# Rotated mixed-chunk keys, 64-column last AV products, spread weight units and later 1/sum transposes in a fused attention and MoE kernel

## Chip, cores and metric

The kernel runs on one core of one Trainium2 chip. The metric is device time in microseconds (us), the median of the runs shown. Times inside a run come from one profiled execution, whose own total is given beside its span.

## What is computed

An attention layer with a learned position bias, followed by two mixture layers. Cut to what matters:

```python
# q, k, v: (4, 8, 576, 64) = batch B, heads H, sequence S, head size D, float32
scores = q @ k.T / 8 + bias                    # bias: a small network of |i-j| and i, one map for each head
attn = exp(scores - max) ; attn /= sum(attn) + 1e-9
x = attn @ v                                   # reshaped to 2304 tokens of 512
h = x @ w_in;  x = (h * relu6(h + 3) / 6) @ w_out             # 512 -> 2048 -> 512
out = (sigmoid(x @ w_gate) * (x @ w_val)) @ w_out2            # 512 -> 1536 -> 512
```

## The kernel before

**Stages.** First the bias maps are built and put in DRAM (lines 540 to 590). Then comes the attention loop (lines 625 to 638), then the two feed-forward layers (from line 650). One unit `n` of attention is a pair of heads of one batch element, so there are 16 units (`NU`).

**Steps and slots.** A unit has nine steps `s` (`NSTEP`). The 576 queries of a head are cut into four chunks of 128 and a rest of 64. Steps 0 to 7 do one chunk `c = s // 2` of one head `h = s % 2`; step 8 does the rests of both heads together, 64 rows each, and is called the mixed chunk here. `slot_of_two(i)` (L463) writes down the work of two steps at a time, and of earlier slots: the scores of slot i, AV products that are due, the exponentials of slot i, `invert` of slot i-1, `turn_inv` of slot i-2, the transposes of slot i-1, and the preparation of the next unit's queries and keys (`prep`, mostly on POOL). The builder then orders each engine's queue itself by readiness and this order, with `tc.issue_after` as an added edge on one engine, so in the trace neighbouring slots interleave.

**One step.** `scores` (L333) makes two halves of 288 keys in one PSUM tile: each half is the sum of two products with a 128x128 query tile as weights, one for the high part of the keys and one for the low part (`r`), and in step 8 of four, as both heads add into one tile (L342). DVE adds the bias and takes the row minimum in one instruction (L346). ACT takes the exponential and the row sum (L362) into `pts`, or for step 8 into `Pm`.

**Transposes.** `trans` (L394) turns the probabilities key-major, four 128x128 blocks into one PSUM tile `tr` (L400; a ring of three), and ACT or DVE evicts them to `ptm`. Head 0 takes keys 0 to 511 this way, head 1 keys 64 to 575. For the mixed chunk the two heads lie in different row halves and start at different columns, so it takes four 64x64 blocks for each head in a `tr` tile of its own, and two evictions (L404 to L410). The 64 keys that are left of each head go through `trans_rem` (L412) into `ptr`: one 128x128 block for each chunk (L415), and two more for the mixed chunk (L418, L419). `Pm` has 64 columns of zeros ahead for this.

**AV.** `av(n, a, g)` (L424) makes the output for 288 queries (`a`). For `g` 0 to 3 there is a product of 64 weight columns for each head, into partitions 0 to 63 and 64 to 127 of one PSUM tile (L432). For `g` 4 one product of 128 weight columns does both heads (L435): the first 64 columns of `v` hold zeros in the rows of the other head, and so on. Each of these plain float32 products shows as two MATMULs in the trace; the scores are float32r and show as one. `av_out` (L437) multiplies by `inv`, with the one PSUM buffer `av`.

**1/sum.** `invert` (L365) adds 1e-9 to the row sums (L368), takes the reciprocal (L369) and spreads it (ACT, L373), after steps 5 and 8. `turn_inv` (L375) transposes that into a `tr` tile (L379) and evicts it to `inv`.

**Weights.** The first ten weight tiles of the next layer are made ready during attention. `load.whole` (L229), in slots 12, 18, ..., 66 (L633), writes down for one tile the DMA of its raw 64-bit words (L159), the absolute value on ACT (L175), four operations on DVE (L176, L184, L186, L188), a copy on ACT (L192) and a subtraction on POOL (L193).

## Time and profile before

| | us |
|---|---|
| median of 3 runs | 1158.08 |
| lowest and highest run | 1157.95, 1161.23 |
| profiled execution, its own time | 1160.52 |
| its span, first to last instruction | 1158.7 |

The mean granted TensorE clock is 0.998 of full speed. Over the span PE is busy for 1135.9 us (98%), weight loads 1012.2 (87%), DVE 772.8 (67%), ACT 588.4 (51%) and POOL 422.6 (36%). The attention loop lies at about 56 to 340 us. PE and PEld are the matmuls and the weight loads of TensorE. A view by line gives the number of instructions, their summed busy time and the mean length of one; as matmuls overlap in the array, the mean is longer than the step from one to the next. The chain of waits gives each piece only the time that it added, and so is read for steps.

### The profile page before, as it was taken

Reading aid. Unit: us, or ns where it says so; the run is one execution under the profiler, and the core shown is the slowest. Engines: PE = TensorE matmul, PEld = TensorE weight load, DVE = VectorE, ACT = ScalarE, POOL = GpSimd, SP = SyncE. Lnnn points to the kernel's source line nnn. Section 1 sums busy time; section 2 is a strip of 40 time slices with the busy share of each in tenths; the row PEclk is TensorE's granted clock in tenths of the full one; section 3 lists DMA queues with packets and bytes.
Section 4 is the critical chain, followed back from the end, with each engine's and each line's share of the span. In section 5 each row is a group of like instructions: output and inputs, shape, how many; then the busy total and the mean of one; then the engine's idle time right before and its main releaser. Section 6 shows DMA issues by size and latency. Waiting matters only on the chain.

```text
span 1158.7 us, 19146 instructions
## 1 busy us (share of the span) xinstructions
PE 1135.9 (98%) x6862; PEld 1012.2 (87%) x6862; DVE 772.8 (67%) x1495; ACT 588.4 (51%) x1296; POOL 422.6 (36%) x342
## 2 busy tenths in 40 slices
PE   8799999999999999999999999999999999999998
PEld 3277777777779999999999999999899898998997
DVE  8977878788868887355386775585367655644443
ACT  7988887877855545454455454342333222221221
POOL 0154544544316433232347445261333223311211
PEclk9999999999999999999999999999999999999999
DMA  6854436353213665249467759976878848757532
GB/s 203 298 162 110 158 95 183 112 165 103 78 55 110 209 218 200 101 174 340 167 228 255 253 189 357 395 261 251 308 254 309 311 165 299 285 181 258 191 109 73
DMA packets 83183, 236.82 MB, mean 204 GB/s; under 512 B 9616, under 2 KB 12304, under 8 KB 83088
## 3 DMA queue, kind: packets, MB, share of 16 engines
q1 hardware_dynamic: 83088, 235.60, 58.6%
q8 instruction: 54, 0.88, 0.3%
q14 instruction: 41, 0.34, 0.1%
HBM read 154.15 MB, written 81.41 MB: 203 GB/s over the span
## 4 chain that ended last, share of the span: by engine, by line
PE 84%; DVE 6%; ACT 2%; DMA 2%; issue 1%; POOL 1%; SPq 0%; POOLq 0%; DVEq 0%; ACTq 0%
PE o L673 17%; PE h L807 10%; PE o L807 10%; PE s L342 6%; PE o L862 6%; PE h L862 5%; PE h L611 5%; PE h L610 5%; PE h L612 5%; PE av L432 5%; PE tr L400 4%; PE av L435 1%; DVE z L186 1%; DVE u L346 1%; PE tr L379 1%
## 5 line engine op out<-in xcount | busy, mean ns | idle before, releaser
L673 PE MATMUL o<-gh,slot 128*128 128x384 f32 x768 | 196.0, 336 | 1.8 <-DVE take L392 1.8
L673 PEld LDWEIGHTS o<-gh,slot 128*128 128x128 f32 x768 | 139.2, 188 | 2.3 <-DVE take L392 2.1
L673 PE MATMUL o<-gl,slot 128*128 128x384 f32 x384 | 129.1, 336 | 0.7 <-DVE gl L659 0.7
L362 ACT ACTIVATE p<-u,stat 128x576 f32<-128x576 f32 x128 | 98.7, 773 | 29.2 <-DVE stat L346 28.4
L342 PE MATMUL s<-k,q 128*128 128x288 f32 x640 | 111.0, 309 | 0.7 <-ACT ptm L557 0.4
L346 DVE CUSTOM_DVE_ANT_0 u<-s,bias 128x576 f32<-128x576 f32 x128 | 93.6, 753 | 24.4 <-PE s L342 23.2
L843 POOL TENSOR_TENSOR gp<-s,gp 128x384 fp32r<-128x384 f32 x36 | 39.4, 1107 | 177.0 <-ACT gp L842 92.6
L617 DVE SCALAR_TENSOR_TENSOR g<-g,h 128x384 f32<-128x384 f32 x94 | 51.6, 549 | 70.2 <-ACT g L616 70.1
L659 DVE TENSOR_TENSOR gl<-g,gh 128x384 fp32r<-128x384 f32 x94 | 63.1, 671 | 48.3 <-ACT gh L658 45.8
L658 ACT CAST gh<-g 128x384 fp32r<-128x384 f32 x94 | 48.3, 513 | 91.6 <-DVE g L617 91.3
L193 POOL TENSOR_TENSOR hl<-corners,hl 128x512 fp32r<-128x512 f32 x42 | 57.2, 1366 | 94.3 <-ACT hl L192 79.3
L342 PEld LDWEIGHTS s<-k,q 128*128 128x128 f32 x640 | 88.8, 189 | 2.3 <-ACT ptm L557 0.6
L616 ACT ACTIVATE g<-h,half 128x384 f32<-128x384 f32 x94 | 54.3, 578 | 58.4 <-PE h L612 57.9
L807 PE MATMUL o<-x,slot 128*128 128x384 f32 x432 | 78.4, 336 | 1.4 <-DVE sum L787 1.4
L432 PE MATMUL av<-ptm,vn 128*64 128x288 f32 x512 | 77.8, 419 | 0.7 <-DVE x L444 0.7
L807 PE MATMUL h<-x,slot 128*128 128x384 f32 x432 | 77.8, 335 | 0.0
L807 PEld LDWEIGHTS o<-x,slot 128*128 128x128 f32 x432 | 75.1, 188 | 2.0 <-DVE sum L787 1.7
L807 PEld LDWEIGHTS h<-x,slot 128*128 128x128 f32 x432 | 75.2, 188 | 0.7
L400 PE MATMUL tr<-ident,p 128*128 128x128 f32 x512 | 72.2, 275 | 2.2 <-ACT inv L390 1.5
L673 PEld LDWEIGHTS o<-gl,slot 128*128 128x128 f32 x384 | 72.5, 189 | 1.3 <-DVE gl L659 1.3
L314 POOL TENSOR_TENSOR k<-early,one 128x576 fp32r<-128x576 f32 x30 | 34.4, 1167 | 106.3 <-DVE x L572 53.1
L843 POOL TENSOR_TENSOR x<-s,x 128x384 fp32r<-128x384 f32 x36 | 40.3, 1129 | 84.2 <-ACT x L842 50.5
(157 smaller groups left out, 2725.2 us busy)
## 6 DMA issues: line engine op xcount, KB each, us to landing
w<-hl SPq DMA_DIRECT2D x67, 512.0 KB, 3.3
slot<-w SPq DMA_DIRECT2D x67, 512.0 KB, 5.8
raw<-in_part_dram SPq DMA_DIRECT2D x50, 512.0 KB, 4.1
x<-xc SPq DMA_DIRECT2D x56, 384.0 KB, 6.0
sum<-sum SPq DMA_DIRECT2D x72, 256.0 KB, 3.5
early<-xc SPq DMA_DIRECT2D x28, 384.0 KB, 6.4
nbias<-ptm SPq DMA_DIRECT2D x36, 295.5 KB, 3.1
early<-in_part_dram SPq DMA_DIRECT2D x32, 288.0 KB, 4.3
```

Of the source, the lines that this page charges most:

```text
L342: last_s[0] = nc.tensor.matmul(ps[:, a, 0:HS], Q[:, q0 : q0 + P], K[:, r, h, HS * a : HS * a + HS], start=(i == 0), stop=(i == len(mm) - 1))
L346: last_u[0] = nc.vector.tensor_tensor_reduce(out=halves(u), in0=ps[:, :, 0:HS], in1=halves(bt), op0=ALU.add, op1=ALU.min, scale=-0.125, sc ...
L362: nc.scalar.activation(probs(t), us.pop(t), AF.Exp, bias=low[n % 2][:, s : s + 1], scale=-1.0, accum_out=sums[n % 3][:, s : s + 1])
L400: nc.tensor.transpose(ps[:, kc], pts[n, c][:, h, 64 * h + P * kc : 64 * h + P * kc + P], ident)
L432: nc.tensor.matmul(ps[64 * h : 64 * h + 64, 0:HS], vt[:, 4 * h + g], ptm[:, h, g, cols], start=(g == 0), stop=False)
L610: nc.tensor.matmul(ps[:, 0:TW], wh, XH[:, c], start=(c == 0), stop=False)
L611: nc.tensor.matmul(ps[:, 0:TW], wl, XH[:, c], start=False, stop=False)
L659: last_g[0] = nc.vector.tensor_tensor(out=gl, in0=g, in1=gh.bitcast(F32), op=ALU.subtract)
L673: nc.tensor.matmul(os[c][:, 0:TW], sl[:, r, P * c : P * c + P], x, start=(first and r == 0 and x is gh), stop=(last and x is gl))
L807: nc.tensor.matmul(ps[b], sl[:, r, o : o + P], x[:, c, s], start=(k < 4 and i == 0), stop=(i == len(mm) - 1), skip_group_check=True)
L843: nc.gpsimd.tensor_tensor(out=G[:, i, 1], in0=s, in1=G[:, i, 0].bitcast(F32), op=ALU.subtract)
L862: nc.tensor.matmul(os[i], x[:, P * i : P * i + P], slots[(base + 14 + e) % NALL][:, r], start=first, stop=last)
```

## The change

There are five edits. The loop has 76 slots (`NSLOT`), the last four only to finish.

1. The bias rows of the mixed chunk's second head are loaded with keys 64 to 575 first and keys 0 to 63 last, and `scores` writes its products in this order (`keys`). In half `a` = 1 a product of 288 keys of head 1 becomes one of 224 and one of 64.
2. With both heads' keys in the same columns, `trans` takes four 128x128 blocks for the mixed chunk, one `tr` tile and one eviction, on DVE and ACT in turn by unit; `trans_rem` takes one block more in place of two, and `Pm` loses its zero columns and their memsets.
3. `av` with `g` = 4 does a product of 64 weight columns for each head.
4. A weight tile's work is spread over six slots from slot 9(m+1)//2 on (`one_step`): DMA; absolute value and maximum; shift; one merge; the other merge; copy and subtraction. The ten tiles start in slots 4, 9, 13, ..., 45.
5. `turn_inv` comes one slot later and first in its slot, and 1e-9 is added as a two-input operation with a tile `tiny`.

```diff
 NPRE = 10
-EVERY = 6
 PRIME = (NU * NSTEP // 2 - 2, NU * NSTEP // 2 + 1)
...
     one = keep.tile([P, 1], F32, name="one")
+    tiny = keep.tile([P, 1], F32, name="tiny")
     slots = [keep.tile([P, 2, 512], F32R, name=f"slot{i}") for i in range(NPRE)]
...
 
+        def shift(self, i):
+            z = self.z[i][0].bitcast(I32)
+            nc.vector.tensor_scalar(out=z, in0=z, scalar1=3, scalar2=0x3FFFFFF8, op0=ALU.logical_shift_left,
+                                    op1=ALU.bitwise_and)
+
+        def merge(self, i, w):
+            z, raw = self.z[i]
+            z = z.bitcast(I32)
+            scalar, op = ((29, ALU.logical_shift_right), (-0x40000000, ALU.bitwise_and))[w]
+            nc.vector.scalar_tensor_tensor(out=z, in0=raw[..., w], scalar=scalar, in1=z, op0=op, op1=ALU.bitwise_or)
+
         def assemble(self, i):
...
             self.raw.pop(i)
-            z, raw = self.z[i]
-            zi = z.bitcast(I32)
-            nc.vector.tensor_scalar(out=zi, in0=zi, scalar1=3, scalar2=0x3FFFFFF8, op0=ALU.logical_shift_left,
-                                    op1=ALU.bitwise_and)
-            nc.vector.scalar_tensor_tensor(out=zi, in0=raw[..., 1], scalar=-0x40000000, in1=zi,
-                                           op0=ALU.bitwise_and, op1=ALU.bitwise_or)
-            nc.vector.scalar_tensor_tensor(out=zi, in0=raw[..., 0], scalar=29, in1=zi,
-                                           op0=ALU.logical_shift_right, op1=ALU.bitwise_or)
+            self.shift(i)
+            self.merge(i, 1)
+            self.merge(i, 0)
 
...
 
-        def whole(self):
-            i = self.n
-            for stage in (self.dma, self.magnitude, self.assemble):
-                stage(i)
-            self.finish(i, nc.gpsimd)
-            self.n += 1
+        def one_step(self, i, k):
+            if k == 0:
+                self.dma(i)
+            elif k == 1:
+                self.magnitude(i)
+                self.raw.pop(i)
+            elif k == 2:
+                self.shift(i)
+            elif k < 5:
+                self.merge(i, 4 - k)
+            else:
+                self.finish(i, nc.gpsimd)
+                self.n = i + 1
 
...
     Ks = [apool.tile([P, 2, 2, S], F32R, name=f"k{i}") for i in range(2)]
-    Pm = [apool.tile([P, S + 64], F32, name=f"pm{i}") for i in range(2)]
+    Pm = [apool.tile([P, S], F32, name=f"pm{i}") for i in range(2)]
     ident = apool.tile([P, P], F32, name="ident")
...
             o = bias_t[c][:, h] if c < 4 else bias_m[64 * h : 64 * h + 64]
-            nc.sync.dma_start(o, rows_of[:, RK * (2 * p + h) : RK * (2 * p + h) + S])
+            i = rows_of[:, RK * (2 * p + h) : RK * (2 * p + h) + S]
+            if c == 4 and h == 1:
+                nc.sync.dma_start(o[:, 0:512], i[:, 64:S])
+                nc.sync.dma_start(o[:, 512:S], i[:, 0:64])
+            else:
+                nc.sync.dma_start(o, i)
 
...
 
+    def keys(s, h, a):
+
+        if s < 8 or h == 0:
+            return [(HS * a, 0, HS)]
+        return [(64, 0, HS)] if a == 0 else [(64 + HS, 0, HS - 64), (0, HS - 64, 64)]
+
     def scores(t):
...
         for a in range(2):
-            mm = [(h, c, r) for h, c in todo for r in range(2)]
-            for i, (h, c, r) in enumerate(mm):
+            mm = [(h, c, r, part) for h, c in todo for r in range(2) for part in keys(s, h, a)]
+            for i, (h, c, r, (k0, o, w)) in enumerate(mm):
                 q0 = (0, S + P)[h] + P * c if c < 4 else (512, S)[h]
-                last_s[0] = nc.tensor.matmul(ps[:, a, 0:HS], Q[:, q0 : q0 + P], K[:, r, h, HS * a : HS * a + HS],
-                                 start=(i == 0), stop=(i == len(mm) - 1))
+                last_s[0] = nc.tensor.matmul(ps[:, a, o : o + w], Q[:, q0 : q0 + P], K[:, r, h, k0 : k0 + w],
+                                             start=(i == 0), stop=(i == len(mm) - 1))
         u = a2.tile([P, S], F32, name="u", bufs=3)
...
             return pts[n, c][:, h]
-        return Pm[n % 2][:, 64:]
+        return Pm[n % 2]
 
...
         r = sums[n % 3][:, 2 * c0 : min(2 * c1, NSTEP)]
-        nc.vector.tensor_scalar(out=r, in0=r, scalar1=1e-9, scalar2=None, op0=ALU.add)
+        nc.vector.tensor_tensor(out=r, in0=r, in1=tiny.to_broadcast(r.shape), op=ALU.add)
         nc.vector.reciprocal(r, r)
...
         else:
-            pm = Pm[n % 2]
-            for h in range(2):
-                ps = pp.tile([P, 4, P], F32, name="tr", bufs=3)
-                r = slice(64 * h, 64 * h + 64)
-                for kc in range(4):
-                    nc.tensor.transpose(ps[:, kc, 0:64], pm[r, 64 + 64 * h + P * kc : 64 + 64 * h + P * kc + P],
-                                        ident[r, r])
-                evac("AV"[h], ptm[:, h, :, 512:S], ps[:, :, 0:64])
+            ps = pp.tile([P, 4, P], F32, name="tr", bufs=3)
+            for kc in range(4):
+                nc.tensor.transpose(ps[:, kc], Pm[n % 2][:, P * kc : P * kc + P], ident)
+            evac("VA"[n % 2], ptm[:, :, :, 512:S], ps.rearrange("p c (h q) -> p h c q", h=2))
 
...
         if c == 3:
-            pm = Pm[n % 2]
-            nc.tensor.transpose(ps[:, 1], pm[:, 0:P], ident)
-            nc.tensor.transpose(ps[0:64, 2], pm[:, S : S + 64], ident)
-            evac("A", ptr[0:64, 512:S], ps[0:64, 2, 0:64])
-            evac("V", ptr[64:P, 512:S], ps[64:P, 1, 64:P])
+            nc.tensor.transpose(ps[0:64, 1], Pm[n % 2][:, 512:S], ident)
+            for h in range(2):
+                evac("AV"[h], ptr[64 * h : 64 * h + 64, 512:S], ps[0:64, 1, 64 * h : 64 * h + 64])
         evac("A", ptr[:, P * c : P * c + P], ps[:, 0])
...
         else:
-            nc.tensor.matmul(ps[:, 0:HS], vt[:, 8:10].rearrange("p a d -> p (a d)"), ptr[:, cols], start=False, stop=True)
+            for h in range(2):
+                nc.tensor.matmul(ps[64 * h : 64 * h + 64, 0:HS], vt[:, 8 + h], ptr[:, cols], start=False, stop=True)
 
...
 
+        for t in steps(i - 3):
+            n, s = seq[t]
+            if s in (5, 8):
+                turn_inv(n, s // 6 * 3, s // 6 * 2 + 3)
         for t in steps(i):
...
                 invert(n, s // 6 * 3, s // 6 * 2 + 3)
-        for t in steps(i - 2):
-            n, s = seq[t]
-            if s in (5, 8):
-                turn_inv(n, s // 6 * 3, s // 6 * 2 + 3)
         for t in steps(i - 1):
...
         nc.vector.memset(one, 1.0)
+        nc.vector.memset(tiny, 1e-9)
         nc.scalar.activation(low[0][:, 0:1], one, AF.Relu)
...
         make_identity(nc, ident)
-        for i in range(2):
-            nc.gpsimd.memset(Pm[i][:, 0:64], 0.0)
 
...
                 begun[f] = hardswish(ring("z")[:, 0:TW], project(0, slots[2 * f], pp.tile([P, 2, 512], F32, name="s")[:, 0]))
-            if i % EVERY == 0 and i > 10 and load.n < NPRE:
-                with tc.issue_after(last_v[0].ins):
-                    load.whole()
+            for m in range(NPRE):
+                at = i - NSTEP * (m + 1) // 2
+                if 0 <= at <= 5:
+                    with tc.issue_after(last_v[0].ins):
+                        load.one_step(m, at)
             if i in PRIME:
...
 

```

## Rows read from the trace of the kernel before

**Rows 1.** Busy time by stretch: PE, PEld, DVE, ACT, POOL, clock, DMA share, GB/s
```profile
73.00:340.00 267.00, 264.19 (x1948) 201.52 (x1946) 209.37 (x540) 210.25 (x551) 121.88 (x92) 1.00 0.40 118
```
**Rows 2.** The page's chain that ended last, by engine
```profile
PE 84%; DVE 6%; ACT 2%; DMA 2%; issue 1%; POOL 1%; SPq 0%; POOLq 0%; DVEq 0%; ACTq 0%
```
**Rows 3.** Instructions by line and shape, PE, 56 to 346 us (busy us, mean ns | idle before)
```profile
L435 PE MATMUL av<-ptr,vn 128*128 128x288 f32 x64 | 24.1, 458 | 0.0
...
L408 PE MATMUL tr<-ident,pm 64*128 64x64 f32 x128 | 10.9, 235 | 0.0
```
**Rows 4.** Chain of waits, 200 to 230 us: AV and its neighbours (start us, us, what)
```profile
200.07 1.02 PE tr L400 x8
...
202.26 0.64 PE av L432 x4
202.90 0.68 PE av L435 x2
203.58 0.87 PE tr L400 x8
...
224.95 1.61 PE av L432 x12
```
**Rows 5.** Chain of waits, 69 to 76 us: mixed chunk transposed in one go
```profile
73.25 0.41 PE tr L408 x8
73.65 0.26 PE tr L415
73.91 0.11 PE tr L418
74.02 0.11 PE tr L419
```
**Rows 6.** Chain of waits, 200 to 230 us: eight whole score products, then a mixed chunk in two goes
```profile
223.90 1.06 PE s L342 x8
...
227.48 0.39 PE tr L408 x4
227.87 0.72 PE s L342 x4
228.59 0.39 PE tr L408 x4
228.98 0.33 PE s L342
229.31 0.11 PE tr L415
...
229.64 0.40 PE s L342 x3
```
**Rows 7.** Who PE waited for, 56 to 346 us (us in total, times, longest)
```profile
PE tr L400 <- ACT inv L390: 1.5, 3, 0.5
PE av L432 <- DVE x L444: 0.7, 3, 0.2
PE tr L400 <- DVE ptm L392: 0.6, 3, 0.2
```
**Rows 8.** Timeline, 122 to 131 us: a merge on DVE beside POOL
```profile
126.39 1.41 POOL L318 TENSOR_TENSOR q<-early,q 64x576 fp32r<-64x576 f32 x1 [2.22 <-ACT q L310]
...
126.44 1.92 DVE L186 SCALAR_TENSOR_TENSOR z<-raw,z 128x512 int32<-128x512 int32 x1
```
**Rows 9.** Instructions by line and shape, DVE, 73 to 340 us
```profile
L368 DVE TENSOR_SCALAR stat<-stat 128x3 f32<-128x3 f32 x15 | 9.2, 613 | 4.8 <-ACT pm L362 4.8
...
L188 DVE SCALAR_TENSOR_TENSOR z<-raw,z 128x512 int32<-128x512 int32 x12 | 8.2, 681 | 0.0
...
L368 DVE TENSOR_SCALAR stat<-stat 128x6 f32<-128x6 f32 x15 | 2.4, 162 | 0.0
```
**Rows 10.** DMA issues, 73 to 340 us (KB each, median us to landing)
```profile
raw<-in_part_dram SPq DMA_DIRECT2D x13, 512.0 KB, 4.0
...
bias_m<-nbias SPq DMA_DIRECT2D x6, 144.0 KB, 5.0
```

## The prediction

> **What bounds the kernel now.** I read the profile from the outside in. The busy time by stretch comes first: in the attention loop's steady part PE is busy for 264.19 of 267 us, while DVE has 209.37 and ACT 210.25, 78% and 79% [rows 1]. The change touches almost nothing outside this loop. The chain that ended last agrees: PE has 84% of the span, DVE 6% and ACT 2% [rows 2]. So the loop lasts as long as PE's queue does, and I ask of each edit what it does to that queue. A list of busy times would mislead here, since matmuls overlap and a change of shape in the array costs time that no instruction owns. So I use the chain of waits over short windows, whose pieces add up to time that passed. The list of waits comes last: PE's own waits in the loop that come back are nine, 1.5 + 0.7 + 0.6 = 2.8 us together [rows 7].
>
> **Edit 3, the last AV product.** Rows 4 show a run of 4 MATMULs of 64 columns (one `g`) in 0.64 and of 12 in 1.61, so four more in a run cost (1.61 - 0.64) / 2 = 0.485. Now, `g` = 3 and 4 take 0.64 + 0.68 for L432 and L435, and the eight transposes behind take 0.87: 2.19. After the change they take 0.64 + 0.485, and transposes that follow 64-column products directly take 1.02 for eight [rows 4]: 2.145. The gain is only 0.045 for each pass, as the switch to another shape moves from ahead of L435 to ahead of the transposes, and does not go. There are 32 passes, L435 having 64 MATMULs in pairs [rows 3].
>
> **Edit 2, the mixed chunk's transposes.** L408 has 128 instructions, eight for each unit [rows 3], and the timeline shows two patterns that alternate by unit. In eight units all eight go in one run behind an AV pass. From its `g` = 3 this costs 0.64 + 0.68 [rows 4] + 0.41 + 0.26 + 0.11 + 0.11 [rows 5] = 2.21. Afterwards it is 0.64 + 0.485, four blocks at 0.87 / 2 = 0.44 plus the 1.02 - 0.87 of a switch behind AV [rows 4], and two blocks of 0.11: 1.935. This saves 0.275, one AV pass included; times eight, 2.2 us. Rows 5 show this pattern. In seven units the two heads go separately, and the second run stands in the middle of the next scores: 0.39 + 0.72 + 0.39 + 0.33 + three times 0.11 (L415 and, as in [rows 5], L418 and L419) + 0.40 = 2.56 [rows 6]. Afterwards it is 0.44 + 0.22 and eight scores in one piece at 1.06 [rows 6]: 1.72, or 1.96 if the scores are still cut once (0.24 more, by the pieces of rows 6). I take a gain of 0.72, times seven, 5.0 us. The last unit stands among AV products; I give it 0.3. The other 24 AV passes give 24 x 0.045 = 1.1. Edits 2 and 3 together: 2.2 + 5.0 + 0.3 + 1.1 = **8.6 us gained**, with bounds of 7.8 and 9.5 from the two ends of the cut scores. The evictions become one of 512 columns in place of two of 256; they run on ACT and DVE, which are idle for a fifth of the loop, so I cost them at nothing. If that cover went, a `tr` tile would come free later; that is rival 3. The dropped memsets were on POOL ahead of the loop; POOL has 1% of the chain [rows 2], so I cost them at nothing too.
>
> **Edit 1, the cut score products.** In each unit two products of 288 columns (`r` = 0, 1) become 224 + 64: 32 more instructions of a kind, float32r under 288 columns, that the trace does not have. Lower bound: the columns are the same in number, so nothing. A middle price: each piece loads 128 weight columns anew, and the shortest step between instructions that do so is 0.11, that of a transpose [rows 5]; two pieces then take 0.22 against 1.06 / 8 = 0.133 for a whole product [rows 6], so 0.09 more each and 2.9 us in all; with 0.133 for each piece it is 4.3 us. Upper bound: such pieces run like plain float32, whose 288 columns take 0.485 in the 64-column shape or 0.68 at L435 [rows 4]: 0.35 to 0.55 more, 11.3 to 17.5 us. I take **3.0 us lost**, since the score products of 288 columns are otherwise in step with their columns, and keep the upper price as a rival. The Trainium skill ("TensorE: Matmul & The Clock Gate", Back-to-back issue gap) prices one product by its moving columns and a fixed few nanoseconds, and says that this under-counts where few columns leave the weight load uncovered. By its formula alone the pieces would cost about 0.1 us in all, an estimate from that page, and the sum would be 3 us better; the 0.11 steps of transposes speak for the caveat.
>
> The mixed chunk's second-head bias comes in two DMAs in place of one: one more for each of four head pairs on SP's queue. They land in 5.0 us [rows 10] and are asked for about a unit ahead; behind them on SP stand later bias, `v` and query loads, as far ahead, so I cost them at nothing.
>
> **Edits 4 and 5, waits.** The nine waits in rows 7 are all releases by DVE or ACT that come late: `inv` and `ptm` evictions that hold a `tr` tile, and the AV product that holds the one `av` buffer. Each comes three times in the loop's 72 slots [rows 7], about as often as a tile's slot (every sixth) and a unit (every 4.5 slots) meet in the same phase, every 18 slots. There four DVE operations of a weight tile crowd one slot, and some are stretched: a merge takes 1.92 beside a POOL operation of 1.41 [rows 8], and 0.68 alone (L188, [rows 9]). Spread over slots, at most about one such operation falls between two score tiles, and the `inv` transposes at a slot's head have the scores behind them as cover. I take all **2.8 us gained**; bounds are 0, and 4.0 (a wait is counted from an instruction's modelled end, and an L408 of 235 ns [rows 3] outlasts its step of 0.39 / 4 [rows 6] by 0.14; nine times that is 1.2). Of the moved step every instruction moves: the DMA on SP (4.0 us to land [rows 10], while ACT reads it at the end of the next slot, and a slot is (340 - 56) / 76 = 3.7 us long; both raw buffers are free by then, so SP does not block), two ACT, four DVE and one POOL operation.
>
> The 1e-9 addition is worth nothing on the path. The three-column form takes 613 ns against 162 for six columns [rows 9], so something holds it; over 16 units that is 16 x 0.45 = 7.2 us of DVE's time, which DVE does not lack. Nor do I expect it back: L186 has two SBUF inputs, as the new form will, and was held in the same way [rows 8]. The Trainium skill speaks against this edit too ("SBUF — State Buffer", Who interferes with whom): a DVE instruction with two SBUF inputs contends with a GpSimd instruction that reads SBUF. By the opposite reading DVE would have 7 us less, and PE's sum stays.
>
> **Sum.** -8.6 + 3.0 - 2.8 = -8.4 us. The profiled execution took 1160.52 (span 1158.7), so it would take 1152.1; it stands 2.4 above the median of 1158.08, so the median would be **1149.7**. This case's own range, from the bounds -9.5 to -7.8, 0 to +4.3 and -4.0 to 0 (sums of -13.5 and -3.5): 1144.6 to 1154.6.
>
> **Rivals.**
> 1. *Narrow float32r pieces run at the plain rate.* For it: no row shows a float32r product under 288 columns, and plain float32 pays 0.485 for the same columns. Against it: nothing in rows 6 hints at such a step. Price 11.3 in place of 3.0: 1158.0, and 1164 at 17.5. Chance 0.22.
> 2. *The slot's head takes back what was gained* (slower). Tile m starts at slot 9(m+1)//2, at the same phase of every unit, and the shift and merges fall two to four slots later, when POOL prepares the next unit's keys. If a held DVE operation meets the same critical eviction each time, ten units have what now three have: a group of waits is 1.3 us (4.0 / 3), so 13.3 in place of 4.0, +9.3. With -5.6 from PE: +3.7, 1161.8. It decides against the change from about 1 us of new waits in each of ten units. Against it: single DVE operations of 0.5 to 1.9 stand beside a slack of a slot. Chance 0.10.
> 3. *The builder cuts the scores again.* The scores stay broken around a full `tr` ring, and the nine waits stay: 2.2 + 7 x 0.3 + 1.4 - 3.0 = 2.7 gained, 1155.4. For it: the ring of three is unchanged, and `turn_inv` is now a burst's last tile. Against it: one tile less for each unit. Chance 0.12.
>
> **How the numbers follow.** The forecast has 0.56. About 0.3%, 3.5 us, is what a measurement of this kernel can tell from no change. Faster by more than that: nearly all of the forecast and a part of rival 3, 0.60. Slower: rival 2 and the upper end of rival 1, 0.13. Within: 0.27. The range goes from 1144.6 to 1159.5: the forecast whole, rival 3, and the likelier part of rival 1; rival 2 and the dear end of rival 1 are left out, under 2 in 10.
>
> **What would show it.** In the new trace: AV as runs of 12 and 8 MATMULs with no other shape between (right if a pass has gained about 0.05); no 64x64 transposes, and mixed-chunk blocks as a run of four at 0.44; eight to ten score pieces of step 8 in about 1.06 + 0.19 (wrong if the chain shows 0.3 or more for each cut product); nine waits gone from PE's list; the addition of 1e-9 still near 0.6 us in some units. The forecast is wrong if the steady part has not lost 5 us or more of its length, or if PE's waits on DVE and ACT come to more than 3 us.

## The result and the profile after

The changed kernel takes **1169.34 us** (median of four runs, 1168.47 to 1170.14) against 1158.53 for the kernel before beside it: a ratio of 1.0089 with a 95% interval of 1.0071 to 1.0106. Forecast were 1149.7 and a range up to 1159.5. The profiled execution took 1169.65, with a span of 1167.8 against 1158.7.

The steady part by stretch, then the chain that ended last by engine, as in rows 1 and 2:

```profile
73.00:340.00 267.00, 258.70 (x1936) 197.06 (x1933) 216.29 (x526) 207.63 (x544) 125.84 (x93) 0.99 0.40 116
```
```profile
PE 79%; DVE 8%; ACT 4%; issue 2%; POOL 1%; DMA 1%; SPq 0%; DVEq 0%; POOLq 0%; ACTq 0%
```

PE was busy for 264.19 of these 267 us [rows 1] and now for 258.70; it had 84% of the chain [rows 2] and has 79%, with the difference on DVE and ACT. A loop that PE's queue set has become one in which PE waits. The instructions by line and shape, PE, 56 to 354 us, show the new shapes:

```profile
L450 PE MATMUL av<-ptm,vn 128*64 128x288 f32 x512 | 79.1, 424 | 0.7 <-ACT ptm L414 0.7
...
L454 PE MATMUL av<-ptr,vn 128*64 128x288 f32 x128 | 21.0, 406 | 0.0
...
L429 PE MATMUL tr<-ident,pm 128*128 128x128 f32 x64 | 10.1, 279 | 0.0
L366 PE MATMUL s<-k,q 128*128 128x224 f32 x32 | 7.8, 307 | 0.0
L366 PE MATMUL s<-k,q 128*128 128x64 f32 x32 | 6.4, 201 | 0.0
```

64 transposes of the mixed chunk stand where 128 of 64x64 stood [rows 3], the last AV products have 64 columns, and each cut has its piece of 224 and of 64. Who PE waits for, 50 to 355 us (us in total, times, longest):

```profile
PE s L366 <- DVE stat L370: 3.9, 5, 3.0
PE tr L403 <- ACT ptm L414: 3.0, 9, 0.4
PE tr L424 <- ACT ptr L414: 2.0, 1, 2.0
PE tr L403 <- DVE ptm L416: 1.5, 4, 0.4
```

The nine waits of rows 7 are gone. In their place come one of 3.0, one of 2.0, thirteen of up to 0.4 ahead of L403 (the moved `turn_inv`), and four small ones ahead of scores (0.9 in all). The 3.0 is at the loop's start. DVE, 54 to 61 us, of before and then of after:

```profile
54.36 0.94 DVE L572 TENSOR_SCALAR x<-x,early 128x576 f32<-128x576 f32 x2
57.76 0.76 DVE L346 CUSTOM_DVE_ANT_0 u<-s,bias 128x576 f32<-128x576 f32 x1 [2.46 <-PE s L342]
```
```profile
55.33 0.43 DVE L176 TENSOR_SCALAR z<-z 128x512 f32<-128x512 f32 x1
55.79 1.25 DVE L180 TENSOR_SCALAR z<-z 128x512 int32<-128x512 int32 x1
57.07 3.46 DVE L187 SCALAR_TENSOR_TENSOR z<-raw,z 128x512 int32<-128x512 int32 x2
60.56 0.76 DVE L370 CUSTOM_DVE_ANT_0 u<-s,bias 128x576 f32<-128x576 f32 x1
```

The first weight tile's four operations are written down in slots 5 to 8, and yet they stand ahead of slot 0's first reduction: the builder orders by readiness, and they were ready. Beside them POOL runs its first key and query operations (from 54.93 on), and two merges take 3.46 in place of twice 0.68 [rows 9]. The first reduction starts at 60.56, not 57.76, and PE waits. The clock follows (PE at this place; then the busy time by stretch, where the granted clock is the last column but two):

```profile
61.39 1.89 PE L366 MATMUL s<-k,q 128*128 128x288 f32 x8 [3.02 <-DVE stat L370]
```
```profile
62.00:66.00 4.00, 4.00 (x21) 3.92 (x20) 2.22 (x6) 3.47 (x10) 3.84 (x3) 0.57 0.68 210
```

After 3.02 us of idling the granted clock is 0.57 over these 4 us, so most of them ran at 1.2 GHz and not 2.4: 21 matmuls where before has 31. The second tile does the same about two units later (DVE, then ACT and PE):

```profile
90.77 0.41 DVE L176 TENSOR_SCALAR z<-z 128x512 f32<-128x512 f32 x1
...
91.22 1.53 DVE L180 TENSOR_SCALAR z<-z 128x512 int32<-128x512 int32 x1
92.79 3.73 DVE L187 SCALAR_TENSOR_TENSOR z<-raw,z 128x512 int32<-128x512 int32 x2
96.44 0.75 DVE L370 CUSTOM_DVE_ANT_0 u<-s,bias 128x576 f32<-128x576 f32 x1
...
97.23 0.22 DVE L416 COPY ptr<-tr 64x64 f32<-64x64 f32 x1
```
```profile
97.48 0.27 ACT L414 COPY ptr<-tr 128x128 f32<-128x128 f32 x1 [0.31 <-DVE ptr L416]
```
```profile
97.80 0.66 PE L424 MATMUL tr<-ident,p 128*128 128x128 f32 x4 [1.98 <-ACT ptr L414]
```

PE wants a `tr` tile. Two evictions still hold it: a 64x64 one that DVE does at 97.23, behind both merges, and one on ACT that comes behind that. Here too the clock falls:

```profile
99.50:103.50 4.00, 4.00 (x19) 2.27 (x18) 1.85 (x6) 2.73 (x9) 0.00 (x0) 0.57 0.00 0
```

**One table.** For each profiled execution I took the loop from its first score product to the first product of the next layer, and added up by how much the step from one PE start to the next exceeds the usual step for the same two shapes (counted from 0.13 us on, so half-clock steps are partly in it). "Work" is the loop without these waits; the next two columns are the lengths of the two layers behind. The split into waits and work is rough: `cut_only` and `cut_only_pinned` issue the same products in another order, and their work differs by 2.2 us, so two rows can be compared to about 2 us. The last column is the median of all runs; single executions differ from it by up to 2 us.

| kernel | loop | waits | work | layer 1 | layer 2 | median |
|---|---|---|---|---|---|---|
| before | 288.6 | 5.5 | 283.1 | 395.9 | 413.3 | 1158.5 to 1159.3 |
| after | 296.2 | 17.5 | 278.7 | 394.4 | 416.0 | 1169.3 |
| `products` | 293.9 | 15.8 | 278.1 | 395.9 | 416.1 | 1168.4 |
| `turn_back` | 295.7 | 16.9 | 278.8 | 395.9 | 416.2 | 1170.4 |
| `spread_later` | 290.6 | 12.9 | 277.7 | 395.8 | 416.1 | 1165.3 |
| `spread_back` | 286.1 | 8.3 | 277.8 | 394.6 | 416.2 | 1159.7 |
| `spread_back_128` | 285.9 | 8.2 | 277.7 | 394.4 | 413.4 | 1156.2 |
| `spread_back_scalar` | 286.5 | 8.8 | 277.7 | 396.0 | 411.5 | 1155.4 |
| `cut_only` | 298.6 | 10.2 | 288.4 | 394.4 | 411.7 | 1168.9 |
| `cut_only_pinned` | 293.3 | 7.1 | 286.2 | 394.4 | 412.0 | 1162.9 |
| `before_pinned` | 289.9 | 6.3 | 283.6 | 394.3 | 413.2 | 1160.0 |
| `products_128_pinned` | 287.6 | 9.9 | 277.6 | 396.1 | 413.4 | 1158.8 |
| `after_128` | 296.5 | 17.8 | 278.7 | 394.5 | 413.6 | 1167.3 |
| `after_128_pinned` | 291.0 | 14.0 | 277.0 | 394.4 | 413.4 | 1161.6 |

From before to after: work -4.4, waits +12.0, layer 1 -1.5, layer 2 +2.7, together +8.8; the spans differ by 9.1. Layer 1 has two lengths. Every execution of the table has a wait of 1.8 us there, at 379 to 393 us. In the six with about 396 us the clock is at half behind it, in the others not (380 to 388 us, before and then `spread_back`):

```profile
380.00:388.00 8.00, 6.23 (x27) 5.81 (x26) 7.26 (x11) 3.19 (x8) 2.44 (x2) 0.79 0.66 230
```
```profile
380.00:388.00 8.00, 7.74 (x44) 7.62 (x45) 7.24 (x13) 4.31 (x9) 2.72 (x2) 1.00 0.83 295
```

What decides it is open; I treat these 1.5 us as chance. The layer 2 of before and of `before_pinned` holds one wait of 1.3 to 1.4 us, and is about 411.8 without it.

### The profile page after: what moved, and what is told of

The parts are those of the page before. It is cut to its first block, busy times and chain, and to the rows that moved or that the text cites. A ratio compares the mean times of both kernels' runs of the same rounds, so it can differ in the third digit from the quotient of the medians.

```text
span 1167.8 us, 19241 instructions
## 1 busy us (share of the span) xinstructions
PE 1138.1 (97%) x6878; PEld 1013.7 (87%) x6878; DVE 783.9 (67%) x1488; ACT 585.6 (50%) x1288; POOL 427.4 (37%) x340
## 4 chain that ended last, share of the span: by engine, by line
PE 79%; DVE 8%; ACT 4%; issue 2%; POOL 1%; DMA 1%; SPq 0%; DVEq 0%; POOLq 0%; ACTq 0%
PE o L693 17%; PE h L827 11%; PE o L827 10%; PE o L882 6%; PE h L882 6%; PE h L630 5%; PE h L628 5%; PE h L629 5%; PE s L366 4%; PE av L450 3%; PE tr L424 3%; DVE u L370 2%; DVE z L187 2%; PE av L454 1%; DVE x L590 1%
## 5 line engine op out<-in xcount | busy, mean ns | idle before, releaser
L366 PE MATMUL s<-k,q 128*128 128x288 f32 (+2 forms) x672 | 112.6, 307 | 4.3 <-DVE stat L370 3.9
L366 PEld LDWEIGHTS s<-k,q 128*128 128x128 f32 x672 | 92.8, 191 | 5.6 <-DVE stat L370 3.3
L424 PEld LDWEIGHTS tr<-ident,p 128*128 128x128 f32 x512 | 56.8, 142 | 26.9 <-issue 19.8
L187 DVE SCALAR_TENSOR_TENSOR z<-raw,z 128x512 int32<-128x512 int32 x76 | 77.6, 1023 | 1.2
L424 PE MATMUL tr<-ident,p 128*128 128x128 f32 x512 | 75.7, 282 | 2.4 <-ACT ptr L414 2.0
```

Source lines behind the costliest of these rows:

```text
L187: nc.vector.scalar_tensor_tensor(out=z, in0=raw[..., w], scalar=scalar, in1=z, op0=op, op1=ALU.bitwise_or)
L366: last_s[0] = nc.tensor.matmul(ps[:, a, o : o + w], Q[:, q0 : q0 + P], K[:, r, h, k0 : k0 + w], start=(i == 0), stop=(i == len(mm) - 1))
L424: nc.tensor.transpose(ps[:, kc], pts[n, c][:, h, 64 * h + P * kc : 64 * h + P * kc + P], ident)
```

## Experiments

### The products alone, and each placement undone

`products` keeps edits 1 to 3 and the 1e-9 form, and puts the loader (whole in one slot, `EVERY` = 6) and `turn_inv` back to their old places. `turn_back` undoes the `turn_inv` move alone, `spread_back` the loader's spreading alone, and `spread_later` starts tile m a unit later:

```diff
-                at = i - NSTEP * (m + 1) // 2
+                at = i - NSTEP * (m + 3) // 2
```

> The changed kernel with edit 4 (spread weight tiles) and the moved 1/sum transposes of edit 5 undone: whole weight tiles in slots 12, 18, ..., 66, and these transposes two slots after their step, behind AV. Edits 1 to 3 and the two-input addition of 1e-9 stay. Theory A (the products gained about 6 us of PE's queue, and the moved steps lost it and more in waits): about 1152 us, 1150 to 1155, with PE's own waits in the loop at 1 to 5 us. Theory B (the cut score products cost 11 us or more): 1163 us or more. Theory C (the other shapes of the products upset the order of the queues by themselves): 1158 us or more, with more than 8 us of waits of PE.

> The changed kernel with only the move of the 1/sum transposes undone (again two slots after their step, behind AV). Theory A: the 13 waits of PE ahead of these transposes, about 0.5 us each, go, and the waits at the start of the loop and near 97 us stay: 1169.3 - 6.6, about 1163 us. If the transposes' place is not a cause: 1168 us or more.

> The changed kernel with only the spreading of weight tiles undone (whole tiles in slots 12, 18, ..., 66). Theory A: the wait of 3.2 us at the loop's start and the one of 2.1 us near 97 us go, with the two drops of the granted clock that follow them (about 1.5 us each), while the 13 waits ahead of the 1/sum transposes stay: 1169.3 - 8, about 1161 us, 1159 to 1163. If the spreading is not a cause: 1168 us or more.

> The changed kernel with each weight tile's six slots nine slots later (slots 13, 18, 22, ..., 54), so that no tile's work can be drawn ahead of the first scores. Theory A: the wait of 3.2 us at the loop's start goes, and the drop of the granted clock after it; the rest stays: 1169.3 - 4.7, about 1164.5 us, and 2 us less if the wait near 97 us belonged to the early tiles too. If it is the spreading as such, whatever its start: 1168 us or more.

Measured, each with its ratio to the kernel before and the 95% interval: `products` 1168.36 (ratio 1.0077, 1.0063 to 1.0090), `turn_back` 1170.41 (1.0100, 1.0086 to 1.0114), `spread_back` 1159.71 (1.0006, 0.9997 to 1.0015), `spread_later` 1165.29 (1.0058, 1.0045 to 1.0072). Work falls by about 5 us in all four; the time doesn't follow it. For `products` theory C came true (15.8 us of waits; B falls by the cut pieces' own steps, below), for `spread_back` and `spread_later` theory A. For `turn_back` it did not: 1163 was expected, and undoing the move made it 1.1 us slower. The spreading costs 9.6 us beside the moved `turn_inv`, and 4.0 of that goes when no tile stands at the loop's start (waits 12.9, and the longest left ahead of scores is 0.5 us). But the products, with the tile `tiny`, lose 9.6 us without any spreading. PE's waits in `products`, 50 to 355 us:

```profile
PE tr L443 <- ACT inv L422: 6.6, 4, 2.4
```

Three of the four are 1.7 to 2.4 us, at 124, 197 and 269 us, one in every fourth unit.

### Is it VectorE's work on the weights?

`products_noz` and `before_noz` leave out the four DVE operations on each of the loop's ten weight tiles (so their times are read without that work).

```diff
         def shift(self, i):
+            if i < NPRE:
+                return
```

> The kernel of the first run (edits 1 to 3 and the two-input addition alone) without the four DVE operations on each of the ten weight tiles of the attention loop, so that these ten tiles hold wrong values; all else is done. Theory E (the waits of PE come from these operations, held on DVE behind POOL and standing ahead of the bias and minimum of the next scores): PE's waits in the loop fall from about 12 us to under 2, the loop ends 12 us earlier, and the time is about 1156 us, with 4.6 of the slower second layer still in it. Rival F (the new products upset PE's queue whatever DVE does): waits of 8 us or more stay and the time is 1165 us or more.

> The kernel before without the four DVE operations on each of the ten weight tiles of the attention loop (these ten tiles hold wrong values; all else is done). Its nine waits of 2.8 to 4.0 us go: about 1155 us under both theories. The difference of its loop's end to that of the run with edits 1 to 3 and the same work left out is what the products save: 6 us if the sums of the prediction hold, 0 or less if the cut scores eat the gain.

Measured: 1163.14 (1.0035, 1.0022 to 1.0048) and 1155.97 (0.9971, 0.9961 to 0.9981). Without this work both get faster, and the products are still 7 us slower. Neither theory met its time (1156, or 1165 and more), but the large waits stay, as rival F has it (`products_noz`, 50 to 355 us):

```profile
PE tr L448 <- ACT inv L427: 8.1, 7, 2.9
```

So DVE's work isn't needed for them. The `inv` eviction on ACT is late for another reason.

### The address

The new tile `tiny` takes 32 bytes in each partition ahead of the weight slots, and every later tile moves by that. The layers behind the loop are not edited, yet their products are slower. PE, 760 to 1130 us, by line and shape: before, after, and below `spread_back_128`, where the tile has 128 bytes:

```profile
L807 PE MATMUL h<-x,slot 128*128 128x384 f32 x387 | 69.8, 335 | 0.0
L862 PE MATMUL o<-slot,gp 128*128 128x512 f32 x144 | 41.0, 391 | 0.0
```
```profile
L827 PE MATMUL h<-x,slot 128*128 128x384 f32 x384 | 70.5, 340 | 0.0
L882 PE MATMUL o<-slot,gp 128*128 128x512 f32 x144 | 41.3, 394 | 0.0
```
```profile
L833 PE MATMUL h<-x,slot 128*128 128x384 f32 x384 | 69.2, 336 | 0.0
...
L888 PE MATMUL o<-slot,gp 128*128 128x512 f32 x144 | 41.2, 393 | 0.0
```

From start to start, the products of `x` with a slot step 176.7 ns on average in after against 173.3 (176.5 in `before_shifted`).

```diff
+    pad = keep.tile([P, 1], F32, name="pad")                       # before_shifted, on before
-    tiny = keep.tile([P, 1], F32, name="tiny")
+    tiny = keep.tile([P, 16], F32, name="tiny")[:, 0:1]            # after_aligned; 32 in place of 16: the _128 kernels
```

> The kernel before with one unused one-column tile beside the small constants, so that every later tile starts 32 bytes later in each partition, as in the changed kernel; the order of all instructions is the same. Theory D: the second mixture layer alone is slower, 1158.6 + 4.6, about 1163.2 us, with 176.7 ns for products that read an x tile. Rival: 1158.6 us.

> The changed kernel with the new one-column tile made 64 bytes long, so that every later tile starts again at a multiple of 64 bytes in each partition, as before the change; the order of all instructions is the same. Theory D (the start of the tiles sets the pace of the second mixture layer, where a product that reads an x tile steps by 176.7 ns in place of 173.3 and the last products by 232 in place of 229): 864 x 3.4 ns + 648 x 2.5 ns = 4.6 us less than the change, about 1164.7 us. Rival (the slower pace comes from elsewhere, such as the order of loads): 1169 us, and the same 176.7 ns.

> The changed kernel with the loader whole again (one weight tile in one slot, as before the change) and the constant tile of 1e-9 made 128 bytes long instead of 32, so that every later tile moves by 128 bytes against the kernel before and not by 32. Layout theory, in the form that the place within 128 bytes relative to x counts: the second mixture layer's products on the slots step 173.3 ns again and not 176.7, its length falls from 416.0 to about 413, the first projection's products gain the same way, and the time falls by 3 to 5 us from 1159.7 to about 1155.5. Rival, that any move of the slots costs (a tile of 64 bytes left the 176): 1159.7 again. If 1155.5, the two layers of the change's body together are worth 3 us over the kernel before, and the change as made loses 10 us through the spreading and 4.5 through the address.

> The changed kernel with the constant tile 128 bytes long, nothing else. Address theory: the second mixture layer's length falls from 416.0 to about 413.4 us, and the rest that moved with it in the runs with the loader whole (1159.7 to 1156.2) as well: 1165 to 1166 against 1169.3. Rival, that the 3.5 us there were of the chance of a draw: 1169.

> The changed kernel with the loader whole again, and with 1e-9 added as before the change, by a scalar instruction and without the constant tile; so nothing moves every later tile. Address theory with a free 1e-9 edit: as the run with the 128-byte tile, 1156.2 within 1 us, the second mixture layer about 413.4 us long. If the constant tile's form spared time beside GpSimd, as its writer may have meant: 1157.5 or more.

Measured: `before_shifted`, in which one unused tile is the only difference, 1162.97 (1.0032, 1.0019 to 1.0045), 4.0 more than the kernel before beside it. `after_aligned` 1168.46 (1.0080, 1.0067 to 1.0093): 64 bytes help little (0.9 us less than after), and the idea that a multiple of 64 was wanted fell. `spread_back_128` 1156.15 (0.9977, 0.9967 to 0.9988), 3.5 us less than with 32 bytes; `after_128` 1167.28 (1.0067, 1.0055 to 1.0080), 2.1 less than after. `spread_back_scalar` adds 1e-9 as before and needs no tile: 1155.37 (0.9968, 0.9957 to 0.9979), the fastest kernel here that does all the work, and 0.3% faster than the kernel before.

So the address is a real term: layer 2 takes 411.5 to 412.0 us without a shift (with the wait of before taken out), about 416 with 32 or 64 bytes, 413.4 with 128. Against no shift the 32 bytes cost some 4 us. The loop's length doesn't change with it (286.1 in `spread_back`, 285.9 in `spread_back_128`). My explanation, the place within 128 bytes, fits the products of `x` only: with 128 bytes they are back at 336 ns, while the 512-column products on the slots stay at 393 (391 without a shift). The rule behind it is open. The form of the 1e-9 addition has no price that these runs can tell: 1155.4 without, 1156.2 with it.

### The order that the builder drew

Is it the cut products? `cut_only` is before with edit 1's cut and nothing else, so with the old addresses.

```diff
+            mm = [(h, c, r, part) for h, c in todo for r in range(2)
+                  for part in (((0, 224), (224, 64)) if s == 8 and h == 1 and a == 1 else ((0, HS),))]
```

> The kernel before with one edit: the second half's mixed score product is cut into 224 and 64 columns. Prices: forecast 0.09 us for each of 32 cuts, 3.0 us, so 1161.7; by the step of the products read in the changed kernel (133 and about 145 ns less the 36 to 40 that the next one gives back) 0.05 each, 1.5 us, so 1160.2. Narrow pieces at the plain rate (the first rival) would be 1164 and more. The layout is the one of before.

Measured: **1168.86** (1.0084, 1.0071 to 1.0097), 10 us lost where 1.5 to 3 were expected. Unit by unit against before, the starts of the score reductions drift by 0.2 to 0.3 us in most units, and by 2.6 from unit 4 to 5, 8 to 9 and 12 to 13 (unit 0 is the first). Those are the units whose start meets the loader's slots 18, 36 and 54. ACT at the first of them, before and then `cut_only`:

```profile
121.27 0.77 ACT L362 ACTIVATE p<-u,stat 128x576 f32<-128x576 f32 x1
...
122.03 0.49 ACT L373 COPY spread<-stat 128x128 f32<-128x128 f32 x2
122.42 0.47 ACT L390 COPY inv<-tr 128x384 f32<-128x384 f32 x1
122.78 0.85 ACT L390 COPY ptm<-tr 128x512 f32<-128x512 f32 x2
123.53 0.69 ACT L175 ACTIVATE z<-raw 128x512 f32<-128x512 f32 x1
```
```profile
121.25 0.69 ACT L175 ACTIVATE z<-raw 128x512 f32<-128x512 f32 x1 [1.01 <-DMA raw<-in_part_dram]
...
122.40 0.78 ACT L363 ACTIVATE p<-u,stat 128x576 f32<-128x576 f32 x1
...
123.93 0.48 ACT L374 COPY spread<-stat 128x128 f32<-128x128 f32 x2
124.32 0.47 ACT L391 COPY inv<-tr 128x384 f32<-128x384 f32 x1
```

In before the loader's absolute value (L175) stands behind the exponentials, the spread copies and the `inv` eviction. In `cut_only` it stands ahead of them all and waits for its DMA; on DVE the same tile's L176 stands ahead of the reciprocal. The `inv` eviction is 1.9 us later, and PE waits for a `tr` tile (PE, 121 to 131 us):

```profile
124.84 0.46 PE L409 MATMUL tr<-ident,pm 64*128 64x64 f32 x4 [1.12 <-ACT inv L391]
```

This wait and one of 0.54 at 129.81 are 1.7 of the unit's 2.6 us; the rest is in no single wait. The edit touches neither ACT line. It can only have changed the builder's reckoning of what is ready when, and with that the order. The test is an added edge that keeps the loader behind the latest reciprocal and spread copy; for the spread loader, each step behind its own slot's reduction and exponential:

```diff
-                with tc.issue_after(last_v[0].ins):
+                with tc.issue_after(last_v[0].ins), tc.issue_after(last_r[0].ins), tc.issue_after(last_p[0].ins):
```

`products_early` and `spread_back_128_early` instead issue the weight tile's DMA one slot ahead:

```diff
+            if i % EVERY == EVERY - 1 and i > 10 and load.n < NPRE:
+                load.dma(load.n)
```

> The products alone (cut score products, whole mixed block, two AV products; loader and 1/sum transposes placed as before the change), with the weight tile's DMA issued one slot ahead of the rest of its work. Theory: the large waits of TensorE (6.6 us in four of them on the 1/sum eviction of ScalarE, 1.8 to 2.6 each) come from ScalarE standing behind the abs that waits for this transfer while a ring of three PSUM tiles is full; with the transfer landed early they shrink to 0.5 each or less, and the time falls by 4 to 7 us from 1168.4 to 1161.5 to 1164.5. Rival, that they come from VectorE's merges held beside GpSimd: nothing changes, 1168. The run that left the VectorE work out (large waits still there at 125.5, 197.5 and 268.0) speaks for the first.

> As the run with the 128-byte tile, and the weight tile's DMA is issued one slot ahead of the rest of its work, so that ScalarE's abs of it no longer stands waiting for the transfer at the head of its queue. If ScalarE behind that transfer is what is left of the loader's price: 1 to 2 us less than the run without it (about 1154). If the 1/sum transposes at the slot's head already took that wait off the path: the same within 0.5 us.

> The kernel before with the cut score products alone, and edges that keep the loader's work behind the latest reciprocal on VectorE and behind the latest spread copy on ScalarE. Drawn-order theory: the 2.6 us in each of units 4, 8 and 12 go, the cuts' own steps stay (0.05 to 0.11 us each, 1.6 to 3.5 us): 1160.5 to 1162.5, against 1168.9 without the edges. Rival, that the cut products themselves cost 10 us (they hold a PSUM tile longer, so that the ring of three fills wherever the edges put the loader): 1167 to 1169.

> The changed products with the loader whole and the 1/sum transposes placed as before the change, with the constant tile 128 bytes long and with the same edges as in the run on the cut products. From 1168.4: the address gives back 4 to 4.5, the waits of 6.6 us on the 1/sum eviction give back 5 to 6: 1157 to 1159. If the edges do nothing: 1164. If the waits only move (ScalarE's later abs delays the loader's slot and with it VectorE's merges): 1160 to 1162.

> The changed kernel with the constant tile 128 bytes long and edges that keep each of the loader's steps behind the score reduction on VectorE and the exponential on ScalarE of its own slot. Drawn-order theory: the late first reduction (60.56 us against 57.76) and the waits of 3.0 us on it go, with the half clock behind them (1.7), and the 2.0 us wait at 97.8 with its half clock (1.7): 8 us less than the run with the 128-byte tile alone, about 1157. If the merges beside GpSimd are what costs, wherever they stand: 1162 or more.

> The kernel before with the edges that keep the loader behind the latest reciprocal and spread copy, nothing else. In the kernel before the order drawn has the loader behind them in units 4, 8 and 12 already, so the drawn-order theory expects no change there: 1158.9 within 1 us; then the cut products cost 3.9 us. If it is 1161 or more, the edges themselves cost, and the cut products only 2 us or less.

Measured, with edges: `cut_only_pinned` 1162.86 (1.0027, 1.0017 to 1.0037), 6.0 less than without; `products_128_pinned` 1158.84 (0.9997, 0.9988 to 1.0006), 9.5 less than `products`, 2 to 3.5 of which are the address; `after_128_pinned` 1161.55 (1.0023, 1.0015 to 1.0032), 5.7 less than `after_128` where 8 or more were expected; `before_pinned` 1160.03 (1.0010, 1.0001 to 1.0019), about 1 us for the edges themselves. ACT and PE of `cut_only_pinned`:

```profile
123.43 0.49 ACT L374 COPY spread<-stat 128x128 f32<-128x128 f32 x2
123.81 0.48 ACT L391 COPY inv<-tr 128x384 f32<-128x384 f32 x1
...
124.93 0.70 ACT L175 ACTIVATE z<-raw 128x512 f32<-128x512 f32 x1
```
```profile
124.35 0.46 PE L409 MATMUL tr<-ident,pm 64*128 64x64 f32 x4
```

The order is back and the wait is gone, with nothing taken out of any engine. So the order is the cause here. It is so in `products` too, which has the same waits in the same units: with the edge its reductions come 2.5, 3.2 and 2.4 us earlier from unit 4 to 5, 8 to 9 and 12 to 13, and its loop is 6.3 us shorter. In `spread_back` the moved `turn_inv` alone does the same, without an edge: the loader's absolute value stands behind the spread copies again (ACT), and the loop is 7.8 us shorter than that of `products`.

```profile
121.95 0.49 ACT L405 COPY spread<-stat 128x128 f32<-128x128 f32 x2
...
123.40 0.68 ACT L176 ACTIVATE z<-raw 128x512 f32<-128x512 f32 x1
```

In the changed kernel the edges take away the two large waits: in `after_128_pinned` the first reduction no longer stands behind the loader (DVE), and PE's longest wait from 56 to 100 us is 0.4.

```profile
56.95 0.76 DVE L370 CUSTOM_DVE_ANT_0 u<-s,bias 128x576 f32<-128x576 f32 x1 [2.48 <-PE s L366]
```

The two runs with the early DMA did the contrary of what I expected: 1175.76 (1.0146, 1.0133 to 1.0159) and 1176.31 (1.0145, 1.0129 to 1.0161). They can't tell about the DMA, since the issue in the slot ahead had no edge of its own. In `products_early` the first two tiles' absolute values run at 20.0 and 27.7 us, ahead of the loop, and the next nine from 76 to 149; `products` has its first eleven from 89 to 309. PE's waits in the loop are about 24 us. On the question they settle nothing, but they show once more that the builder takes whatever is ready.

What the edges leave of the spreading's price, 1161.55 against 1156.15 with the loader whole, is waits again (14.0 against 8.2). About half of the difference stands ahead of `turn_inv`, at a `tr` ring still held by an ACT eviction (first line: `after_128_pinned`; second: `spread_back_128`). Why these evictions come late I didn't test; no run has the edges, the spread loader and the old `turn_inv` together.

```profile
PE tr L403 <- ACT ptm L414: 5.8, 12, 0.7
```
```profile
PE tr L411 <- ACT ptm L422: 3.0, 10, 0.4
```

## Why the prediction was wrong

**What bounds the loop, edits 2 and 3: right.** From `cut_only_pinned` to `products_128_pinned` PE's work falls from 286.2 to 277.6 us. These 8.6 are the 8.6 forecast, to the 2 us that the table can tell. The last two AV groups and eight transposes behind them take 2.05 us from start to start (medians) where before took 2.10: the 0.05 forecast for a pass. Of the 8.6 the time kept 4.0 (medians). In the profiled executions it is 2.8: 2.8 us went into waits, 1.7 into layer 1's chance and 1.4 into layer 2, by the address of the 128-byte tile.

**Edit 1: the size right.** Work rises by 2.6 from `before_pinned` to `cut_only_pinned`, the medians by 2.8; 3.0 was forecast. By their own steps (0.146 and 0.036 us) the two pieces take 0.18 us against 0.133 for the whole product, 1.6 us in 32 cuts, where 0.22 was reckoned; the other 1.0 is within what the table can tell. Rival 1 (11.3 and more) falls: the pieces aren't at the plain rate. By the formula of the Trainium skill ("TensorE: Matmul & The Clock Gate", Back-to-back issue gap) the estimate was about 0.1 us for all cuts, and its caveat says that the formula under-counts products of few columns. The 1.6 us by the steps agree with the caveat.

So edits 1 to 3 are worth -8.6 + 2.6 = -6.0 of work, against -5.6 in the sum.

**Edits 4 and 5, the waits: the step that failed.** The term of 2.8 us gained became 12.0 us of new waits (5.5 to 17.5 in the table). Two reasons behind it were wrong. That "at most about one such operation falls between two score tiles" takes the slots in which work is written down for the times at which it runs: the builder ran a tile's four operations in one piece, 5.2 us at 55 and 5.7 us (with one reciprocal between) at 91. And that DVE and ACT "are idle for a fifth of the loop", for which edit 2's evictions were costed at nothing, is an average: at 92.79 two merges hold back the one eviction that PE needs. Nor did the sum ask what the products by themselves do to the order, which cost `products` its gain (15.8 us of waits). The spreading costs 11.1 us (`spread_back_128` to `after_128`), and 5.4 with edges. The half that was right is `turn_inv` at the slot's head, but only with the loader whole: 1168.36 to 1159.71 us (`products` to `spread_back`). Beside the spread loader its undoing costs 1.1 us.

**Left out: the address, a second term put at nothing.** Edit 5's addition was called "worth nothing on the path". Its instruction is; its 32 bytes cost 4.0 us against no tile (`before_shifted`), and 2.1 against a tile of 128 bytes (3.5 beside the whole loader). The statement that the operation stays held is right: L392's three-column form now takes 895 ns on average and the six-column form 415, against 613 and 162 [rows 9].

```profile
L392 DVE TENSOR_TENSOR stat<-stat,tiny 128x3 f32<-128x3 f32 x16 | 14.3, 895 | 5.0 <-ACT pm L386 4.8
...
L392 DVE TENSOR_TENSOR stat<-stat,tiny 128x6 f32<-128x6 f32 x15 | 6.2, 415 | 0.1
```

In after, all fifteen additions of more than 0.7 us have a POOL instruction beside them and end within 0.03 us of the end of one; without one beside them none takes more than 0.17. The Trainium skill ("SBUF — State Buffer", Who interferes with whom) says that a DVE instruction with two SBUF inputs contends with a GpSimd instruction that reads SBUF, and the trace agrees. But in before the one-input form was held in the same way, 0.85 to 1.15 us in seven of its additions, and its six-column ones never met POOL. So the longer means don't show what the second input does by itself.

**The rivals.** Rival 2 had the sign and the engine (the loader's held operations take back the gain), with 1161.8 for a chance of 0.10. Its place was off: not one wait of 1 us in each of ten units, but 3.0 and 2.0 us in two places, both with a half clock behind, and thirteen small ones at `turn_inv`. Rival 3 named the ring of three and `turn_inv` as a burst's last tile; L403 does split the scores in after (one score product of eight behind it at 93.43, five at 99.34). Its price of 1155.4 left out that a full ring also waits for an eviction behind the loader.

**The sum by runs** (medians): edges +1.1 (`before_pinned`), cuts +2.8, AV and mixed chunk -4.0 (with 1.4 of the 128-byte address in it), `turn_inv` at the head in place of the edges -2.7, spreading +11.1, address from 128 to 32 bytes +2.1: +10.4. A chain of runs comes out at the difference of its ends in any case, so this is an account and no proof, and its terms hang on its order. A range built on bounds for each edit left out what all edits do together, a new order and new addresses.

## What to carry to other kernels

- Where a builder orders the queues by readiness, the slot in which work is written down is not when it runs. A filler needs an edge behind the work that PE waits for, on each engine that it uses; otherwise any edit, even of another line, can put it ahead.
- Before costing a small edit, look at what it allocates. A tile of a few bytes ahead of matmul operands moves them all, which cost 4 us here in a stage that wasn't edited. Doing without the tile avoids it (`spread_back_scalar`); putting it last wasn't tried.
- Compare first where the units drift, then look at the queues of one unit that does.

## What was not expected of the hardware

- One idle wait of PE of 3.02 us was followed by 4 us at a granted clock of 0.57; the 2.0 us wait at 97.8 likewise (0.57 from 99.5 to 103.5). The 1.8 us wait in layer 1 was followed by half clock in some executions and in others not.
- PE's products on the same shapes step 173.3 ns or about 176.6 by the addresses of their operands alone (before, `before_shifted`).
